# Moving an untaken path's transfers to another engine, and two steps inside a kernel's tail

## The chip, the cores and the metric

The kernel runs on one core of one Trainium2 chip. The metric is the device time of one execution in microseconds (us), given as the median of three timed runs. A profile of one more execution shows what each engine did: PE (TensorE), DVE (VectorE), ACT (ScalarE), POOL (GpSimd) and SP (SyncE), which only issues transfers and waits. Every engine has an instruction stream of its own; they meet through semaphores.

## The reference

Block-sparse attention, and behind it a layer with softmax times its input, a layer norm and a product. With q, k, v of 4 batches x 8 heads x 768 x 64, and x of 3072 tokens x 512:

```python
mask = |blk_i - blk_j| <= 1, or first or last block, or a sampled block   # blocks of 32
attn = softmax(where(mask, q @ k.T / 8, -1e9));  x = attn @ v             # heads side by side
h = x @ w_in                                       # 512 -> 1024
solu = h * softmax(h)
ln = (solu - mean(solu)) / sqrt(var(solu) + 1e-6) * g_ln
out = ln @ w_out                                   # 1024 -> 512, float32
```

## The kernel before

**The fast path.** The work is cut into 12 passes of two tiles of 128 queries over all heads. In each pass PE makes scores (L416), ACT takes the exponential without a maximum (L427), PE multiplies with v and a column of ones (L444), DVE divides (L457, L458). The 24 tiles of 128 tokens then go through the layer: PE makes h (L487), ACT e = exp(h) with its sum (`e_exp`, L496), DVE solu = h * e (`solu`, L508), the statistics of solu in two halves (`stats`, L522), and the small steps es, mv and vpe (`rstd`, L529, L532, L538); POOL raises vpe to the power -1/2 (L540). PE multiplies the turned solu by a centred w_out (L547), ACT or DVE scales the product by rstd (`scaled`) and a transfer stores it (`store`, L563).

**The order.** Nothing here is ordered by a scheduler. Each step is put into a list with a due time by `at`, and `emit` issues the list sorted by time; each engine's queue has that order. The end of the kernel, from `end`, is a list written out by hand (L937 to L973): its entries are issued one after the other. In it, pass LP - 1 is the last but one and LP the last; each has tiles 0 and 1. The last tile (LP, 1) is the end of the chain: `solu`, the turn by PE (`ln_mm`, L877), the copy (`ln_out`), the product in two halves of 256 columns (`o_half`, L893: `oe1a` and `oe1b`, eight matmuls each), the scaling of the halves by DVE and ACT (`scale_half`, L905 and L902), and two stores, one issued by SP and one by ACT.

**The flag.** The fast path is right only where no sum leaves a range. `check_r` and `check_e` (L915, L916) compare the reciprocals and the sums of all tiles with bounds, `check_sum` counts what is in range (L926) and makes `bad` (L927), one value for each partition; `check_bad` adds these up with a matmul of one column (L932, float32) and DVE writes the sum as an integer, `bad_i` (L933).

**The If.** All five engines load `bad_i` into a register (L985) and compare it with zero (L986):

```python
n_bad = nc.values_load(bad_i[0:1, 0:1], min_val=0, max_val=128)
with tc.If(n_bad > 0):
    general_path(tc, q, k, v, sampled_blocks, w_in_sb, w_out_sb, ident, out)
```

With these inputs the flag is zero, and every engine branches past its part of `general_path`, a slow version of the whole computation in loops (L57 to L205). Behind it stand waits and resets of semaphores (also L986), the wait of SP for all semaphores, and the barriers that end the program (L1012). L1001 is the start: a few register moves and fills, and a barrier that POOL opens.

Of the kernel before, what the change touches and what calls it, by code (L numbers as in the profile page):

```python
# [7 lines left out]
FP32 = mybir.dt.float32  # L8
# [7 lines left out]
def block_mask(nc, m_sb, m_ps, sampled_blocks, NB, neg):  # L16

    NR = sampled_blocks.shape[1]
    maskT = m_sb.tile([NB, NB], FP32, name="maskT")
    nc.vector.memset(maskT, 0.0)  # L20
    for fill, base, cm, step in (
        (neg, 1, -1, 1), (neg, 1, 1, -1),
        (0.0, -1, 1, 0), (0.0, NB - 2, -1, 0),
        (0.0, -1, 0, 1), (0.0, NB - 2, 0, -1),
    ):
        nc.gpsimd.affine_select(out=maskT, in_=maskT, compare_op=ALU.is_ge, fill=fill,
                                base=base, channel_multiplier=cm, pattern=[[step, NB]])
    _t = sampled_blocks.tensor
    _t32 = bass.DRamTensorHandle(_t.name, (2 * NB * NR,), I32)
    samp_flat_ap = bass.AP(tensor=_t32, offset=0, ap=[[0, 1], [1, 2 * NB * NR]])  # L30
    samp_i = m_sb.tile([1, NB * NR, 2], I32, name="samp_i")
    nc.sync.dma_start(out=samp_i.rearrange("a b c -> a (b c)"), in_=samp_flat_ap)
    ones1 = m_sb.tile([1, NB], BF16, name="ones1")
    nc.vector.memset(ones1, 1.0)
    samp_lo_bf = m_sb.tile([1, NB * NR], BF16, name="samp_lo_bf")
    nc.vector.tensor_copy(out=samp_lo_bf, in_=samp_i[:, :, 0])
    samp_ps = m_ps.tile([NB, NB, NR], FP32, name="samp_ps")
    nc.tensor.matmul(samp_ps.rearrange("a b c -> a (b c)"), ones1, samp_lo_bf,
                     start=True, stop=True)
    samp_f = m_sb.tile([NB, NB, NR], FP32, name="samp_f")  # L40
    nc.scalar.copy(out=samp_f, in_=samp_ps)
    kb_iota_i = m_sb.tile([NB, 1], I32, name="kb_iota_i")
    nc.gpsimd.iota(kb_iota_i, pattern=[[0, 1]], base=0, channel_multiplier=1)
    kb_iota = m_sb.tile([NB, 1], FP32, name="kb_iota")
    nc.vector.tensor_copy(out=kb_iota, in_=kb_iota_i)
    eq = m_sb.tile([NB, NB, NR], FP32, name="eq")
    nc.vector.tensor_scalar(out=eq, in0=samp_f, scalar1=kb_iota, scalar2=None, op0=ALU.is_equal)
    anyeq = m_sb.tile([NB, NB], FP32, name="anyeq")
    nc.vector.reduce_sum(out=anyeq, in_=eq, axis=AX.X)
    nc.vector.tensor_scalar(out=anyeq, in0=anyeq, scalar1=-1.0, scalar2=1.0,  # L50
                            op0=ALU.mult, op1=ALU.add)
    nc.vector.tensor_scalar(out=anyeq, in0=anyeq, scalar1=0.0, scalar2=None, op0=ALU.max)
    nc.vector.tensor_mul(out=maskT, in0=maskT, in1=anyeq)
    return maskT


def general_path(tc, q, k, v, sampled_blocks, w_in_sb, w_out_sb, ident, out):  # L57

    nc = tc.nc
    B, H, S, D = q.shape  # L60
    BLK = 32
    NB = S // BLK
    TQ = 128
# [3 lines left out]
    KD, KF, d_ff = w_in_sb.shape[1], w_out_sb.shape[1], w_in_sb.shape[2]  # L67
    with tc.tile_pool(name="f_c", bufs=1) as f_c, \
         tc.tile_pool(name="f_dram", bufs=1, space=bass.MemoryType.DRAM) as f_dram:
        x_scr = f_dram.tile([B, S, H * D], BF16, name="x_scr")  # L70
        m_scr = f_dram.tile([NB, S], BF16, name="m_scr")
        qT = f_c.tile([TQ, TQ], BF16, name="f_qT")
        kT = f_c.tile([TQ, S], BF16, name="f_kT")
        with tc.tile_pool(name="f_m", bufs=1) as f_m, \
             tc.tile_pool(name="f_mp", bufs=1, space=bass.MemoryType.PSUM) as f_mp:
            maskT = block_mask(nc, f_m, f_mp, sampled_blocks, NB, -1e30)
            sel = f_m.tile([NB, NB, BLK], FP32, name="sel")
            nc.vector.memset(sel, 0.0)
            nc.gpsimd.affine_select(out=sel, in_=sel, compare_op=ALU.not_equal, fill=1.0,
                                    base=0, channel_multiplier=1, pattern=[[-1, NB], [0, BLK]])  # L80
            for t in (qT, kT):
                nc.vector.memset(t[D:TQ, :], 0.0)
            nc.vector.tensor_copy(out=kT[D : D + NB, :].rearrange("p (q o) -> p q o", o=BLK),
                                  in_=sel)
            m_row = f_m.tile([NB, NB, BLK], BF16, name="m_row")
            nc.vector.tensor_copy(
                out=m_row,
                in_=maskT.rearrange("p (q o) -> p q o", o=1).broadcast_to([NB, NB, BLK]))
            nc.sync.dma_start(out=m_scr, in_=m_row.rearrange("p q o -> p (q o)"))
        with tc.tile_pool(name="f_sb", bufs=2) as f_sb, \  # L90
             tc.tile_pool(name="f_ps", bufs=1, space=bass.MemoryType.PSUM) as f_ps:
            with tc.For_i(0, B, 1) as b:
                with tc.For_i(0, H, 1) as h:
                    kc = f_sb.tile([TQ, NCH, D], BF16, tag="f_k")
                    vc = f_sb.tile([TQ, NCH, D], BF16, tag="f_v")
                    for dst, src in ((kc, k), (vc, v)):
                        nc.gpsimd.dma_start(
                            out=dst, in_=src[bass.ds(b, 1), bass.ds(h, 1), :, :].rearrange(
                                "a e (c p) d -> p (a e c) d", p=TQ))
# [5 lines left out]
                    with tc.For_i(0, S, TQ) as t0:  # L105
                        qc = f_sb.tile([TQ, D], BF16, tag="f_q")
                        nc.gpsimd.dma_start(
                            out=qc, in_=q[bass.ds(b, 1), bass.ds(h, 1), bass.ds(t0, TQ), :].rearrange(
                                "a e p d -> p (a e d)"))
                        nc.sync.dma_start(out=qT[D : D + NB, :], in_=m_scr[:, bass.ds(t0, TQ)])  # L110
                        tq = f_ps.tile([D, TQ], BF16, tag="f_tq")
                        nc.tensor.matmul(tq, qc, ident, is_transpose=True, start=True, stop=True)
                        nc.vector.tensor_copy(out=qT[0:D, :], in_=tq)
# [1 line left out]
                        for i in range(2):  # L115
                            nc.tensor.matmul(sp[:, i, 0:384], qT, kT[:, i * 384 : (i + 1) * 384],
                                             start=True, stop=True)
# [5 lines left out]
                        p = f_sb.tile([TQ, 2, 384], BF16, tag="f_p")  # L123
# [12 lines left out]
                        for j in range(NCH):  # L136
# [4 lines left out]
                        xo = f_sb.tile([TQ, D], BF16, tag="f_x")  # L141
                        nc.vector.tensor_scalar(out=xo, in0=op, scalar1=rs, scalar2=None,
                                                op0=ALU.mult)
                        nc.sync.dma_start(
                            out=x_scr[bass.ds(b, 1), bass.ds(t0, TQ), bass.ds(h * D, D)].rearrange(
                                "a p d -> p (a d)"),
                            in_=xo)
# [1 line left out]
        with tc.tile_pool(name="f_sb2", bufs=2) as f_sb, \  # L149
             tc.tile_pool(name="f_ps2", bufs=1, space=bass.MemoryType.PSUM) as f_ps:  # L150
            with tc.For_i(0, n_tok, 128) as t0:
                xt = f_sb.tile([128, d_model], BF16, tag="f_xt")
                nc.sync.dma_start(out=xt, in_=x_rows[bass.ds(t0, 128), :])
                tps = f_ps.tile([128, KD, 128], BF16, tag="f_tps")
                for c in range(KD):
                    nc.tensor.matmul(tps[:, c, :], xt[:, c * 128 : (c + 1) * 128], ident,
# [45 lines left out]
                                     stop=(c == KF - 1))  # L202
                ot = f_sb.tile([128, d_model], FP32, tag="f_ot")
                nc.scalar.copy(out=ot, in_=ops)
                nc.sync.dma_start(out=out[bass.ds(t0, 128), :], in_=ot)  # L205


@with_exitstack
def kernel(
# [11 lines left out]
    nc = tc.nc  # L221
# [5 lines left out]
    TQ = 128  # L227
# [346 lines left out]
    with tc.manual_schedule():  # L574
# [309 lines left out]

        o2 = {}

        def o_half(half, pool, tag):
            if pool is p_sco:
                o2[half] = p_sco.tile([128, 2, HF], FP32, tag=tag, name="oe1a")[:, 0, 0:256]
            else:  # L890
                o2[half] = pool.tile([128, d_model], FP32, tag=tag, name="oe1b")[:, 0:256]
            for c in range(KF):
                nc.tensor.matmul(o2[half], lnT_of[LP, 1][:, c, :],  # L893
                                 w_cen_sb[:, c, half * 256 : (half + 1) * 256],
                                 start=(c == 0), stop=(c == KF - 1), skip_group_check=True)
# [13 lines left out]
        def tile_in(pool, tag, name):  # L909
            if pool is p_sco:  # L910
                return lambda: p_sco.tile([128, 2, HF], FP32, tag=tag, name=name)[:, 0, :]
            return lambda: pool.tile([128, d_model], FP32, tag=tag, name=name)
# [12 lines left out]
        def check_sum():  # L925
            nc.vector.reduce_sum(out=n_ok[:, 0:1], in_=okr, axis=AX.X)  # L926
            nc.vector.tensor_scalar(out=bad, in0=n_ok[:, 0:1], scalar1=float(n_r + n_e),  # L927
                                    scalar2=None, op0=ALU.is_lt)

        def check_bad():  # L930
            bad_ps = p_h.tile([1, 1], FP32, tag="h", name="bad_ps")
            nc.tensor.matmul(bad_ps, bad, ones_c, start=True, stop=True)  # L932
            nc.vector.tensor_copy(out=bad_i, in_=bad_ps)  # L933

        end = SLOTS * NPASS
        A, V = nc.scalar, nc.vector
        for n, (fn, *args) in enumerate((  # L937
            (h_end, 0, 2, KD),
            (e_exp, LP, 0),
            (o_mms, LP - 1, 0, 5, 8),  # L940
            (scaled, LP - 1, 0, A),
            (store, LP - 1, 0),
            (stats, LP - 1, 1),
            (rstd, LP - 1, 1),
            (check_r, n_r - 2 * PC, n_r),
            (h_end, 1, 0, KD),
            (solu, LP, 0),
            (e_exp, LP, 1),
            (o_mms, LP - 1, 1, 0, 3, tile_in(p_op, "op", "o_10")),
            (ln_mm, 0),  # L950
            (ln_out, 0, A),
            (o_mms, LP - 1, 1, 3, 8),
            (solu, LP, 1),
            (check_e,),
            (stats, LP, 0),
            (rstd, LP, 0),
            (o_mms, LP, 0, 0, 2, tile_in(p_sco, "sco", "oe0")),
            (ln_mm, 1),
            (ln_out, 1, A),
            (stats, LP, 1),  # L960
            (rstd, LP, 1),
            (o_mms, LP, 0, 2, 8),
            (scaled, LP - 1, 1, A),
            (store, LP - 1, 1),
            (check_sum,),
            (scaled, LP, 0, A),
            (store, LP, 0),
            (o_half, 0, p_sco, "sco"),
            (o_half, 1, p_op, "op"),
            (scale_half, 0, V, nc.sync),  # L970
            (scale_half, 1, A, nc.scalar),
            (check_bad,),
        )):  # L973
            at(end + 0.01 * n, fn, *args)
        at(end - 5.0, x_turn, LP, 0, 2)
# [41 lines left out]
```

## Time and profile before

| | us |
|---|---|
| timed runs | 213.96 median (213.76 to 214.35) |
| the profiled execution | 213.1 |
| its span, first to last instruction | 211.5 |
| PE, ACT, DVE, POOL busy | 199.9, 174.5, 139.9, 107.4 |
| granted clock of PE, mean | 0.989 |

The span leaves out what lies around the program in an execution. Of a row of a timeline, the first number is the start in us from the span's start, the second the duration; square brackets hold the idle time of the engine before it and what ended it. A "q" behind an engine's name is its sequencer: waits, branches, register loads and the issuing of transfers, which aren't counted as busy. In rows that list one line, "17/30/43" is the shortest, median and longest duration in ns, and two start times follow. EVENT_SEMAPHORE is a wait, a reset, or both; it is recorded when it is done, with some 20 ns. DMA queues q8 and q14 hold the fetches of instructions.

### The profile page before, as it was taken

Reading aid. Unit: us, or ns where it says so; the run is one execution under the profiler, and the core shown is the slowest. Engines: PE = TensorE matmul, PEld = TensorE weight load, DVE = VectorE, ACT = ScalarE, POOL = GpSimd, SP = SyncE. Lnnn points to the kernel's source line nnn. Section 1 sums busy time; section 2 is a strip of 40 time slices with the busy share of each in tenths; the row PEclk is TensorE's granted clock in tenths of the full one; section 3 lists DMA queues with packets and bytes.
Section 4 is the critical chain, followed back from the end, with each engine's and each line's share of the span. In section 5 each row is a group of like instructions: output and inputs, shape, how many; then the busy total and the mean of one; then the engine's idle time right before and its main releaser. Section 6 shows DMA issues by size and latency. Waiting matters only on the chain.

```text
span 211.5 us, 5629 instructions
## 1 busy us (share of the span) xinstructions
PE 199.9 (95%) x2238; PEld 137.5 (65%) x2238; DVE 139.9 (66%) x329; ACT 174.5 (82%) x208; POOL 107.4 (51%) x155
## 2 busy tenths in 40 slices
PE   7989999999989999999999999999999999999950
PEld 2669867776666677677667667567667667664530
DVE  5895879988647656656655755756745845768760
ACT  6988989889869889889888988888988988784640
POOL 7989698679494264689334355699111011011120
PEclk9999999999999999999999999999999999999995
DMA  6999999899999799997798899896706507462230
GB/s 173 338 360 217 379 376 273 166 243 271 194 301 203 180 258 237 274 192 203 193 299 154 189 311 261 199 269 127 206 3 149 81 24 124 125 83 76 79 149 11
DMA packets 73907, 42.03 MB, mean 199 GB/s; under 512 B 55828, under 2 KB 69396, under 8 KB 73876
## 3 DMA queue, kind: packets, MB, share of 16 engines
q1 hardware_dynamic: 72932, 40.06, 77.9%
q0 software_dynamic: 528, 1.05, 2.6%
q10 hardware_dynamic: 416, 0.52, 0.9%
q8 instruction: 18, 0.29, 0.6%
q14 instruction: 13, 0.11, 0.2%
HBM read 23.07 MB, written 6.29 MB: 139 GB/s over the span
## 4 chain that ended last, share of the span: by engine, by line
PE 74%; DVE 8%; DMA 7%; POOL 3%; issue 2%; ACT 2%; ACTq 0%; POOLq 0%; DVEq 0%
PE sco L416 25%; PE h L487 15%; PE op L444 15%; PE o L547 13%; DMA pd<-nat 5%; DMA xT<-xb 2%; DVE stats L522 2%; POOL KT L327 2%; PE warm_t L403 2%; DVE solu L508 2%; PE he L867 1%; DVE QT L664 1%; POOL QT L327 1%; PE mean_ps L750 1%; PE tp_k L346 1%
## 5 line engine op out<-in xcount | busy, mean ns | idle before, releaser
L427 ACT ACTIVATE exs<-sco 128x1024 bf16<-128x1024 f32 x144 | 140.4, 1024 | 9.4 <-PE sco L416 6.9
L416 PE MATMUL sco<-QT,KT 88*128 88x256 bf16 x576 | 86.9, 272 | 1.1 <-POOL QT L327 0.5
L416 PEld LDWEIGHTS <-KT 88*128 88x128 bf16 x576 | 54.2, 97 | 32.9 <-issue 6.6
L487 PE MATMUL h<-w_in_sb,xT 128*128 128x512 bf16 x176 | 55.3, 379 | 0.3 <-DMA xT<-xb 0.3
L444 PE MATMUL op<-VA,exs 128*128 128x65 bf16 x1152 | 51.8, 194 | 0.0
L444 PEld LDWEIGHTS <-exs 128*128 128x128 bf16 x1152 | 48.5, 97 | 3.7 <-DVE xb L458 0.3
L547 PE MATMUL o<-w_cen_sb,lnT 128*128 128x512 bf16 x176 | 45.2, 379 | 0.0
L540 POOL TENSOR_TENSOR rstd<-vpe,mhalf 128x1 f32<-128x1 f32 x24 | 13.2, 548 | 54.9 <-DVE vpe L538 49.5
L457 DVE RECIPROCAL recip_all<-op 128x4 f32<-128x4 f32 x48 | 8.7, 182 | 42.8 <-PE op L444 42.7
L496 ACT ACTIVATE e<-h 128x1024 bf16<-128x1024 f32 x22 | 22.5, 1023 | 12.9 <-PE h L487 11.5
L522 DVE BATCH_NORM_STATS2 stats<-solu 128x6 f32<-128x512 bf16 x48 | 30.6, 680 | 0.0
L327 POOL COPY KT<-pd 64x768 bf16<-64x768 bf16 x24 | 20.1, 837 | 16.5 <-DMA pd<-nat 15.7
L508 DVE TENSOR_TENSOR solu<-h,e 128x1024 bf16<-128x1024 f32 x22 | 26.8, 1216 | 1.6 <-ACT e L496 1.6
L547 PEld LDWEIGHTS <-lnT 128*128 128x128 bf16 x176 | 15.9, 98 | 13.8 <-DMA lnT<-solu 0.2
L558 DVE TENSOR_SCALAR ot<-o,rstd 128x512 f32<-128x512 f32 x20 | 15.0, 751 | 10.8 <-issue 5.3
L458 DVE TENSOR_TENSOR xb<-op,recip_all 128x256 bf16<-128x256 f32 x48 | 20.4, 424 | 1.7
L327 POOL COPY QT<-pd 64x768 bf16<-64x768 bf16 x24 | 19.7, 821 | 1.0
L487 PEld LDWEIGHTS <-xT 128*128 128x128 bf16 x176 | 16.0, 98 | 5.2 <-DMA xT<-xb 1.5
L327 POOL CAST nat<-st_q 128x768 bf16<-128x768 f32 (+2 forms) x19 | 13.6, 714 | 8.1 <-DMA st_q<-in_q_dram 8.0
L327 POOL CAST VA<-st_v 128x768 bf16<-128x768 f32 x16 | 13.1, 828 | 7.7 <-DMA st_v<-in_v_dram 3.9
L327 POOL CAST nat<-st_k 128x768 bf16<-128x768 f32 x15 | 12.7, 846 | 4.9 <-DMA st_k<-in_k_dram 4.6
L740 POOL TENSOR_SCALAR w_out_sb<-w_out_f,g_ln_sb 128x512 bf16<-128x512 f32 x8 | 6.0, 759 | 2.1 <-DMA w_out_f<-in_moe_w_out_dram 2.1
(89 smaller groups left out, 113.5 us busy)
## 6 DMA issues: line engine op xcount, KB each, us to landing
st_v<-in_v_dram SPq DMA_DIRECT2D x16, 384.0 KB, 5.0
out_dram<-ot SPq DMA_DIRECT2D x23, 256.0 KB, 2.6
st_k<-in_k_dram SPq DMA_DIRECT2D x15, 384.0 KB, 5.5
st_q<-in_q_dram SPq DMA_DIRECT2D x12, 384.0 KB, 6.5
w_out_f<-in_moe_w_out_dram SPq DMA_DIRECT2D x4, 512.0 KB, 7.6
st_q<-in_q_dram SPq DMA_DIRECT2D x4, 256.0 KB, 6.9
w_in_sb<-in_moe_w_in_dram POOLq DMA_DIRECT2D x1, 1024.0 KB, 11.9
st_q<-in_q_dram SPq DMA_DIRECT2D x4, 128.0 KB, 4.7
```

The lines of the kernel that those rows point to most:

```text
L327: eng.tensor_copy(out=o, in_=i)
L416: nc.tensor.matmul(sco[:, hh, kk * QW : (kk + 1) * QW], KT[b % 2][0:KR, h * NCH + 2 * u + kk, :], QT[b % 2][0:KR, h * NCH + PC * j : h * N ...
L427: nc.scalar.activation(out=exs_of[ps, pr][:, u].rearrange("p a b c -> p (a b c)"), in_=sco_of.pop(s).rearrange("p a b -> p (a b)"), func=A ...
L444: nc.tensor.matmul(op[:, hh, ic, :], exs[:, u, hh, kk, ic * TQ : (ic + 1) * TQ], VA[b % 2][:, 2 * pr + hh, 2 * u + kk, :], start=(u == 0 a ...
L458: nc.vector.tensor_tensor(out=xb_of[ps][:, pr].rearrange("p c (h d) -> p h c d", h=2), in0=op[:, :, :, 0:D], in1=recip.broadcast_to([TQ, 2 ...
L487: nc.tensor.matmul(h_of[ps, i][:, half, :], xT_of[ps][:, c * PC + i, :], w_in_sb[:, c, half * HF : (half + 1) * HF], start=(c == 0), stop= ...
L496: nc.scalar.activation(out=o, in_=h, func=ACT.Exp, scale=1.0, accum_out=esum_all[:, t : t + 1])
L508: nc.vector.tensor_mul(out=so, in0=h, in1=e)
L522: nc.vector.bn_stats(out=stat_of[ps, i][:, half, :], in_=so[:, half, :])
L540: nc.gpsimd.tensor_tensor(out=rstd_of[ps, i], in0=vpe, in1=mhalf, op=ALU.pow)
L547: nc.tensor.matmul(ops_of[ps, i], lnT_of[ps, i][:, c, :], w_cen_sb[:, c, :], start=(c == 0), stop=(c == KF - 1), skip_group_check=True)
L558: nc.vector.tensor_scalar(out=o, in0=i_, scalar1=r, scalar2=None, op0=ALU.mult)
```

## The change

Three edits.

1. Six transfers of `general_path` and `block_mask` are issued by POOL instead of SP: the sampled blocks, the mask's two, the loop's store of x, the second loop's load and its store. They aren't executed with these inputs.
2. In the list of the end, the statistics of tile (LP, 0) go ahead of the last `solu`, the steps of its rstd follow that solu at once, then the statistics and rstd of the last tile, then `check_e` and `check_sum`.
3. `check_bad` is cut in two: its matmul stands between the fifth and the sixth matmul of `oe1b`, and the copy to `bad_i` behind DVE's scaled half.

```diff
-    nc.sync.dma_start(out=samp_i.rearrange("a b c -> a (b c)"), in_=samp_flat_ap)
+    nc.gpsimd.dma_start(out=samp_i.rearrange("a b c -> a (b c)"), in_=samp_flat_ap)
...
-            nc.sync.dma_start(out=m_scr, in_=m_row.rearrange("p q o -> p (q o)"))
+            nc.gpsimd.dma_start(out=m_scr, in_=m_row.rearrange("p q o -> p (q o)"))
...
-                        nc.sync.dma_start(out=qT[D : D + NB, :], in_=m_scr[:, bass.ds(t0, TQ)])
+                        nc.gpsimd.dma_start(out=qT[D : D + NB, :], in_=m_scr[:, bass.ds(t0, TQ)])
...
-                        nc.sync.dma_start(
+                        nc.gpsimd.dma_start(
                             out=x_scr[bass.ds(b, 1), bass.ds(t0, TQ), bass.ds(h * D, D)].rearrange(
...
-                nc.sync.dma_start(out=xt, in_=x_rows[bass.ds(t0, 128), :])
+                nc.gpsimd.dma_start(out=xt, in_=x_rows[bass.ds(t0, 128), :])
...
-                nc.sync.dma_start(out=out[bass.ds(t0, 128), :], in_=ot)
+                nc.gpsimd.dma_start(out=out[bass.ds(t0, 128), :], in_=ot)
...
-        def o_half(half, pool, tag):
-            if pool is p_sco:
+        def o_half(half, pool, tag, c0=0, c1=KF):
+            if c0:
+                pass
+            elif pool is p_sco:
...
-            for c in range(KF):
+            for c in range(c0, c1):
...
         def check_bad():
-            bad_ps = p_h.tile([1, 1], FP32, tag="h", name="bad_ps")
-            nc.tensor.matmul(bad_ps, bad, ones_c, start=True, stop=True)
-            nc.vector.tensor_copy(out=bad_i, in_=bad_ps)
+            bad_ps.append(p_h.tile([1, 1], FP32, tag="h", name="bad_ps"))
+            nc.tensor.matmul(bad_ps[0], bad, ones_c, start=True, stop=True)
+
+        def check_out():
+            nc.vector.tensor_copy(out=bad_i, in_=bad_ps[0])
...
             (solu, LP, 0),
+            (stats, LP, 0),
             (e_exp, LP, 1),
             (o_mms, LP - 1, 1, 0, 3, tile_in(p_op, "op", "o_10")),
             (ln_mm, 0),
             (ln_out, 0, A),
             (o_mms, LP - 1, 1, 3, 8),
             (solu, LP, 1),
-            (check_e,),
-            (stats, LP, 0),
             (rstd, LP, 0),
+            (stats, LP, 1),
             (o_mms, LP, 0, 0, 2, tile_in(p_sco, "sco", "oe0")),
             (ln_mm, 1),
             (ln_out, 1, A),
-            (stats, LP, 1),
             (rstd, LP, 1),
+            (check_e,),
+            (check_sum,),
             (o_mms, LP, 0, 2, 8),
             (scaled, LP - 1, 1, A),
             (store, LP - 1, 1),
-            (check_sum,),
             (scaled, LP, 0, A),
             (store, LP, 0),
             (o_half, 0, p_sco, "sco"),
-            (o_half, 1, p_op, "op"),
+            (o_half, 1, p_op, "op", 0, 5),
+            (check_bad,),
+            (o_half, 1, p_op, "op", 5, KF),
             (scale_half, 0, V, nc.sync),
+            (check_out,),
             (scale_half, 1, A, nc.scalar),
-            (check_bad,),
```

Lines behind the diff's third part are two to eight higher after: L915 is L917, L893 is L895, L932 is L936, L933 is L939, L985 is L993, L986 is L994, L1012 is L1020.

What the compiled programs hold between an engine's branch at the If and its target, and behind the target to the end, counted in their lists of instructions:

| | passed over, before | after | behind the target, before | after |
|---|---|---|---|---|
| SP | 137 | 110 | 21 | 17 |
| POOL | 126 | 154 | 11 | 14 |
| DVE | 128 | 136 | 5 | 5 |
| ACT | 105 | 113 | 5 | 5 |
| PE | 197 | 205 | 5 | 5 |

The program's start differs too: register moves ahead of the first barrier are four on SP and three on POOL before, none and five after. At the end SP's list of waits for semaphores has ten entries before and twelve after, POOL's waits at the If two and five; the six that SP has at the If before are gone after.

More of the change, by code (lines that the diff above doesn't have):

```diff
@@ L928, in check_sum @@
                                     scalar2=None, op0=ALU.is_lt)
+        bad_ps = []
         def check_bad():
-            bad_ps = p_h.tile([1, 1], FP32, tag="h", name="bad_ps")
-            nc.tensor.matmul(bad_ps, bad, ones_c, start=True, stop=True)
-            nc.vector.tensor_copy(out=bad_i, in_=bad_ps)
+            bad_ps.append(p_h.tile([1, 1], FP32, tag="h", name="bad_ps"))
+            nc.tensor.matmul(bad_ps[0], bad, ones_c, start=True, stop=True)
+        def check_out():
+            nc.vector.tensor_copy(out=bad_i, in_=bad_ps[0])
         end = SLOTS * NPASS
```

## The prediction

> **What bounds the kernel now.** I read the page first, for the span, then the timeline of the last ten microseconds, then the rows of the lines that end the program. From the page:
>
> ```profile
> span 211.5 us, 5629 instructions
> ```
>
> The profiled execution took 213.1 us, 1.6 us more than its span, and the median of the three timed runs is 213.96. I make the sum against the span and take what it changes from the median.
>
> The change touches the first half microsecond, the last ten, and a path that isn't run. Up to 195 us both kernels issue the same work in the same order, so the end is where to look. The timeline there, cut to what the argument needs (start, duration, engine, line, operation):
>
> ```profile
> 196.12 1.22 DVE L508 TENSOR_TENSOR solu<-he,e 128x1024 bf16<-128x1024 f32 x1 [0.15 <-ACT e L496]
> 198.50 1.23 DVE L508 TENSOR_TENSOR solu<-he,e 128x1024 bf16<-128x1024 f32 x1 [1.15 <-ACT e L496]
> 199.84 0.18 DVE L916 SCALAR_TENSOR_TENSOR okr<-esum_all,okr 128x24 f32<-128x24 f32 x1
> 199.94 1.28 DVE L522 BATCH_NORM_STATS2 stats<-solu 128x6 f32<-128x512 bf16 x2
> 201.50 0.16 DVE L538 TENSOR_TENSOR vpe<-es,mv 128x1 f32<-128x1 f32 x1
> 201.57 1.28 DVE L522 BATCH_NORM_STATS2 stats<-solu 128x6 f32<-128x512 bf16 x2
> 202.57 1.04 PE L893 MATMUL oe1b<-w_cen_sb,lnTe 128*128 128x256 bf16 x8
> 203.20 0.16 DVE L538 TENSOR_TENSOR vpe<-es,mv 128x1 f32<-128x1 f32 x1
> 203.28 0.37 DVE L926 TENSOR_REDUCE n_ok<-okr 128x1 f32<-128x216 f32 x1
> 203.50 0.55 POOL L540 TENSOR_TENSOR rstd<-vpe,mhalf 128x1 f32<-128x1 f32 x1 [1.16 <-DVE vpe L538]
> 203.68 0.15 DVE L927 TENSOR_SCALAR bad<-n_ok 128x1 f32<-128x1 f32 x1
> 203.98 0.19 PE L932 MATMUL bad_ps<-ones_c,bad 128*1 128x1 f32 x2 [0.38 <-DVE bad L927]
> 204.09 0.47 ACT L902 ACTIVATE ot_last<-oe1b,rstd 128x256 f32<-128x256 f32 x1 [1.02 <-POOL rstd L540]
> 204.09 0.48 DVE L905 TENSOR_SCALAR ot_last<-oe1a,rstd 128x256 f32<-128x256 f32 x1 [0.25 <-POOL rstd L540]
> 204.49 0.13 DVE L933 CAST bad_i<-bad_ps 1x1 int32<-1x1 f32 x1
> 204.59 0.38 ACTq L563 DMA_DIRECT2D out_dram<-ot_last  x1
> 204.60 0.33 SPq L563 DMA_DIRECT2D out_dram<-ot_last  x1
> ```
>
> DVE runs without a gap from 198.50 to 203.84; the last tile's rstd ends at 204.05 because two pairs of statistics stand behind the last solu. PE has finished the last product at 203.61, and ACT stands idle 1.02 us for rstd. So up to 204.6 DVE's queue is the limit. But 6.9 us of span are left, and in them no engine computes. The waits of SP's own queue, then the rows of line 986 (the If), of the two register loads that count, and of line 1012 (the end of the program):
>
> ```profile
> SPq L986 <- SPq L986: 3.6, 1, 3.6
> ```
>
> ```profile
> L986 SPq EVENT_SEMAPHORE  x6: 17/17/17, 209.5 to 209.9; - x6
> L986 POOLq EVENT_SEMAPHORE  x2: 17/30/43, 205.7 to 205.8; - x2
> L986 POOLq COMPARE_BRANCH  x1: 45/45/45, 205.2 to 205.2; - x1
> L986 DVEq COMPARE_BRANCH  x1: 72/72/72, 205.3 to 205.3; - x1
> L986 ACTq COMPARE_BRANCH  x1: 54/54/54, 205.7 to 205.7; - x1
> L986 DVEq EVENT_SEMAPHORE  x1: 21/21/21, 205.9 to 205.9; - x1
> L986 SPq COMPARE_BRANCH  x1: 53/53/53, 205.9 to 205.9; - x1
> L986 POOLq INC_SWDGE_SEM  x1: 206/206/206, 205.9 to 205.9; - x1
> L986 ACTq EVENT_SEMAPHORE  x1: 17/17/17, 206.2 to 206.2; - x1
> ```
>
> ```profile
> L985 POOLq TENSOR_LOAD <-bad_i x1: 503/503/503, 204.7 to 204.7; - x1
> L985 SPq TENSOR_LOAD <-bad_i x1: 544/544/544, 205.0 to 205.0; - x1
> ```
>
> ```profile
> L1012 SPq EVENT_SEMAPHORE  x12: 17/28/28, 210.0 to 211.5; - x12
> L1012 SPq DRAIN  x3: 7/7/13, 210.6 to 211.0; - x3
> ```
>
> Every engine loads the flag, branches past the general path and goes on behind it. POOL, DVE and ACT are there 0.5 us after their branch. **SP branches at 205.9 and does its next instruction at 209.5.** It waits for no transfer: stores take at most 2.0 us to land, so the one issued at 204.59 is in by 206.6.
>
> ```profile
> DMA to landing us min/median/max: 1.8/2.0/2.0
> ```
>
> From 210.0 SP walks ten waits in 0.6 us, 0.06 each; then 0.9 us of barriers end the span. What sets the end is SP's jump.
>
> The DMA view, for 204.5 to 207.6 us (two rows) and for 207.6 to the end (one), shows what runs meanwhile:
>
> ```profile
> q14 instruction: 4, 0.03, 4.1%
> q8 instruction: 1, 0.02, 2.3%
> ```
>
> ```profile
> q14 instruction: 1, 0.01, 0.5%
> ```
>
> Five instruction fetches follow the five jumps; a sixth comes alone near SP's resumption. That fits a jump that left what SP had loaded, so that it had to wait for its target. The lengths fit too: the jumps of ACT, POOL and DVE pass over 105, 126 and 128 instructions (the table in the section on the change) and cost 0.5 us or less, SP's passes over 137 and costs 3.6. Fetches on q14 are 8 KB each (0.03 MB in four), on q8 16 KB. How many instructions that is, two lines of the page tell:
>
> ```profile
> PE   199.9 (95%) x2238; PEld 137.5 (65%) x2238; DVE 139.9 (66%) x329; ACT 174.5 (82%) x208; POOL 107.4 (51%) x155
> q8 instruction: 18, 0.29, 0.6%
> ```
>
> Only PE has a program so long: its 4476 instructions in 18 fetches make about 250 for 16 KB, so about 125 for 8 KB.
>
> **The change part by part.** *Transfers of the general path.* None is executed, so none costs time as a transfer. What moves is program length: SP's jump shrinks from 137 to 110 instructions, POOL's grows from 126 to 154, DVE's from 128 to 136. SP's 110 is near ACT's 105, so I take its jump at 0.5 us (bounds 0.4 and 3.6). POOL's 154 isn't in the trace: from below 0.4, its own jump of 126; from above 3.6, SP's of 137. It lies nearest, and beyond, the jump that stalled, so **I take 3.6 us on POOL**. DVE's 136 is one short of 137; I take 3.6 there as well, hidden as shown below.
>
> [...]
>
> *Start.* SP issues register moves ahead of the first barrier, and POOL issues three; POOL gets two more and SP loses its four.
>
> ```profile
> L1001 SPq MOVE  x4: 29/34/42, 0.0 to 0.2; - x4
> L1001 POOLq MOVE  x3: 29/29/39, 0.1 to 0.3; - x3
> ```
>
> POOL's moves start some 0.06 apart, and POOL opens the barrier: +0.1 us on everything (bounds 0 and 0.2).
>
> *Statistics ahead of the last solu.* The first solu ends at 197.34. Its statistics, 1.28, now fill the gap in which DVE waited for e: 197.4 to 198.65. The last solu can start some 0.08 before that end, as pipelined neighbours do here: 198.57 instead of 198.50. PE's last products shift by this 0.07 (bounds 0 and 0.2). Behind the solu come es, mv and vpe of the last but one tile (0.45), then the last tile's statistics from 200.15, es, mv, vpe (201.77 in place of 203.20): **rstd 1.43 us earlier**, 202.07 to 202.62. The checks of esum (0.4), the reduce and the comparison follow, and bad is there near 202.8 (before: 203.83).
>
> *The flag's sum inside the last products.* PE reaches it after five of eight matmuls of oe1b, near 203.2, so bad is 0.4 us early; if it were late, three matmuls and ACT's store would wait with it. The two f32 matmuls delay those three by 0.05 to 0.25; I take 0.15. oe1b ends near 203.83, ACT scales at once and issues its store at 204.36 in place of 204.59. DVE's half needs rstd and oe1a, whose last matmul ends with oe1b's first ones (202.8): scaled by 203.33, SP's store at 203.35 in place of 204.60. bad_i is written by 203.57, in place of 204.62: 1.05 earlier.
>
> *The end, added up.* POOL's load starts 0.04 after bad_i: 203.62, branch done at 204.2. With the stall it goes on at 207.8. It then has five waits where it had two, at about 0.09 each, and INC_SWDGE_SEM: 0.7, to 208.5. SP has been behind its own branch since 205.2 but its first end wait is for a semaphore that this instruction raises. Twelve waits of 0.06 follow (0.75), then 0.9: 210.15, and 210.25 with the start. DVE, if it stalls, is back at 207.9; the last store has landed by 206.4; both lie under POOL. The span changes by 210.25 - 211.5 = -1.25 us. From the median: **212.7 us**.
>
> **The rivals.**
>
> *No jump stalls.* What counts would be how many block ends lie within the jump, and not its length. With blocks of about 125 a jump of 137 passes two ends in some 12 positions of 125, one of 154 in some 29: POOL would be spared in three of four cases. For it: the fetches come in whole blocks. Against it: that SP had one of 12 positions in 125 would be chance, whereas length explains all four rows. [...] The end is then the last store, landed at 206.4; SP has seven waits left (0.45), then 0.9 and 0.1: 207.85, 3.65 us less, 210.3 us. If DVE alone stalled, SP would meet its semaphore at 207.9: five waits, 0.9 and 0.1 give 209.2, 211.7 us.
>
> *SP stalls all the same (the move does nothing).* The cause would be something else that only SP has, such as the two operations of line 985 between load and branch. Its flag load follows its store, 203.7 rather than 205.0; the branch ends at 204.7, it is back at 208.3, twelve waits, 0.9 and 0.1: 210.05, -1.45, 212.5 us.
>
> *Slower: POOL stalls twice.* POOL has some fourteen instructions behind its target. If a block ends within them, the next block is asked for only at resumption (the lone sixth fetch stands near SP's resumption, too), and POOL pays a second 3.6 ahead of its INC_SWDGE_SEM, with SP and the barrier behind it: -1.25 + 3.6 = +2.35, 216.3 us. It decides from the point where a second stall costs more than 1.25 us. Against it: 14 positions of 125, and SP with 21 instructions behind its target shows one stall.
>
> **How the numbers follow.** POOL stalls once: 0.55. No stall 0.25, with DVE alone in it. SP stalls all the same 0.09. POOL twice 0.05. The rest, 0.06, is for a tail that gives back what I count, about no change. The range 209.9 to 213.3 holds the first three, with 0.4 us on either side for the starting moves, PE's two matmuls and a stall a little longer than SP's, and leaves out 0.11 to 0.2. About 0.3% (0.64 us) is what a measurement of this kernel can tell from no change; the forecast's -1.25 lies beyond it, and needs a stall of over 4.2 us to fall inside. Faster 0.86, same 0.08, slower 0.06.
>
> **What would show it.** Line 994 (the If) after: SP's waits begin 0.5 us after its branch, or they don't; POOL's first wait stands 3.6 us after POOL's branch, or 0.4; DVE's likewise. rstd of the last tile ends near 202.7, bad_i near 203.7, ACT's last store starts near 204.5 (each with the 0.1 of the start). SP's end waits begin near 208.6. If POOL doesn't stall I am wrong by 2.4 us to the long side; if bad comes after PE's fifth matmul, PE has a gap ahead of line 936.

## The result, and the profile after

| | before | after |
|---|---|---|
| median of seven runs, us | 213.96 (213.15 to 214.98) | 211.82 (210.41 to 212.45) |
| ratio after/before | | 0.9884, 95% interval 0.9848 to 0.9919 |
| the profiled execution, us | 213.1 | 210.96 |
| its span, us | 211.5 | 209.2 |

The kernel became 1.2% faster by the ratio, which is that of the means; by the medians it is 1.0%. The forecast said 212.7 in a range of 209.9 to 213.3, so the time lies where it was expected; the way there was another one. Page of the profile after, its first line:

```profile
span 209.2 us, 5592 instructions
```

The If after the change (line 994; it was 986):

```profile
L994 POOLq EVENT_SEMAPHORE  x5: 17/43/43, 204.8 to 205.2; - x5
L994 POOLq COMPARE_BRANCH  x1: 45/45/45, 204.4 to 204.4; - x1
L994 DVEq COMPARE_BRANCH  x1: 72/72/72, 204.4 to 204.4; - x1
...
L994 SPq COMPARE_BRANCH  x1: 53/53/53, 204.7 to 204.7; - x1
...
L994 DVEq EVENT_SEMAPHORE  x1: 21/21/21, 205.0 to 205.0; - x1
L994 POOLq INC_SWDGE_SEM  x1: 195/195/195, 205.2 to 205.2; - x1
```

POOL branches at 204.4 and does its next instruction at 204.8; DVE takes 0.6 us. **No jump stalls**, though POOL's passes over 154 instructions. SP's waits at the If are gone; what it does behind its branch stands in the row of the program's end, and its waits tell where it stood longest:

```profile
L1020 SPq EVENT_SEMAPHORE  x14: 17/28/28, 205.4 to 209.2; - x14
...
L1020 SPq DRAIN  x3: 7/7/13, 208.4 to 208.7; - x3
```

```profile
SPq L1020 <- DMA out_dram<-ot_last: 2.2, 1, 2.2
SPq L1020 <- PEq L1020: 0.7, 2, 0.5
SPq L1020 <- remote: 0.6, 1, 0.6
```

The 0.6 us on `remote` end when POOL's INC_SWDGE_SEM is done (205.2 and 0.195 us). SP begins its end waits then, at 205.4, and could be through by 206.1. It stands 2.2 us in one of them, for a store of `ot_last`, until 207.9; seven waits and the barriers follow. So the last store ends this kernel. When was it issued? The tail's timeline:

```profile
202.00 0.57 POOL L540 TENSOR_TENSOR rstd<-vpe,mhalf 128x1 f32<-128x1 f32 x1 [1.15 <-DVE okr L917]
...
202.61 0.15 DVE L929 TENSOR_SCALAR bad<-n_ok 128x1 f32<-128x1 f32 x1
...
203.13 0.19 PE L936 MATMUL bad_ps<-ones_c,bad 128*1 128x1 f32 x2
...
203.26 0.50 PE L895 MATMUL oe1b<-w_cen_sb,lnTe 128*128 128x256 bf16 x3
203.27 0.33 SPq L563 DMA_DIRECT2D out_dram<-ot_last  x1
203.36 0.15 DVE L939 CAST bad_i<-bad_ps 1x1 int32<-1x1 f32 x1
203.84 0.47 ACT L904 ACTIVATE ot_last<-oe1b,rstd 128x256 f32<-128x256 f32 x1 [1.14 <-issue]
204.35 0.37 ACTq L563 DMA_DIRECT2D out_dram<-ot_last  x1
```

ACT issues it at 204.35 and it lands at 207.9, 3.5 us later; before, the same store was issued at 204.59 and landed at 206.62 by the trace's landing records, 2.0 us later. The transfers of the changed kernel in two stretches, 205.45 to 206.4 and 206.4 to 207.9 us (packets, MB, share of the 16 DMA engines). q10 is ACT's queue, which carries only this store here, in 128 packets of 1 KB and 16 of 4 bytes; q14 and q8 carry instructions:

```profile
q10 hardware_dynamic: 70, 0.06, 19.2%
q14 instruction: 4, 0.03, 12.9%
q8 instruction: 1, 0.02, 7.8%
```

```profile
q10 hardware_dynamic: 15, 0.01, 7.0%
```

Five instruction fetches, as many as there are jumps, run among the store's packets from 205.49 on, and 15 packets start only when all five fetches have started (the fifth at 206.38), the last at 207.3. In the kernel before, the same two queues between 205.6 and 206.3, and between 206.3 and 207.6:

```profile
q10 hardware_dynamic: 144, 0.13, 53.9%
```

```profile
q14 instruction: 4, 0.03, 9.8%
q8 instruction: 1, 0.02, 5.4%
```

There all 144 packets are through, the last at 206.28, before the first fetch starts at 206.35. In the changed kernel bad_i comes at 203.51 in place of 204.62, the first branch at 204.36 in place of 205.23, the first fetch at 205.49 in place of 206.35, and so among the packets of the store.

### The profile page after: what moved, and what is told of

Same layout as the page of the kernel before. It is cut to its first block, busy times and chain, and to the rows that moved or that the text cites. A ratio compares the mean times of both kernels' runs of the same rounds, so it can differ in the third digit from the quotient of the medians.

```text
span 209.2 us, 5592 instructions
## 1 busy us (share of the span) xinstructions
PE 198.0 (95%) x2204; PEld 137.3 (66%) x2238; DVE 140.1 (67%) x329; ACT 174.7 (84%) x208; POOL 107.7 (51%) x155
## 4 chain that ended last, share of the span: by engine, by line
PE 71%; DMA 9%; POOL 8%; DVE 5%; issue 3%; ACT 1%; POOLq 0%
PE sco L416 24%; PE op L444 15%; PE o L547 13%; PE h L487 13%; DMA pd<-nat 7%; POOL KT L327 3%; DMA xT<-xb 2%; POOL QT L327 2%; PE he L867 1%; POOL nat L670 1%; DVE QT L664 1%; PE oe L547 1%; PE mean_ps L750 1%; DVE xb L458 1%; POOL nat L327 1%
## 5 line engine op out<-in xcount | busy, mean ns | idle before, releaser
L487 PE MATMUL h<-w_in_sb,xT 128*128 128x512 bf16 x153 | 48.6, 378 | 0.7 <-DMA xT<-xb 0.2
L547 PE MATMUL o<-w_cen_sb,lnT 128*128 128x512 bf16 x166 | 43.2, 379 | 0.5
L327 POOL CAST nat<-st_q 128x768 bf16<-128x768 f32 (+2 forms) x19 | 14.3, 752 | 9.8 <-DMA st_q<-in_q_dram 9.4
L327 DVE COPY QT<-tp_q 64x256 bf16<-64x256 bf16 (+1 forms) x16 | 5.6, 351 | 1.4 <-PE tp_q L356 1.1
```

The source lines that it names most:

```text
L327: eng.tensor_copy(out=o, in_=i)
L487: nc.tensor.matmul(h_of[ps, i][:, half, :], xT_of[ps][:, c * PC + i, :], w_in_sb[:, c, half * HF : (half + 1) * HF], start=(c == 0), stop= ...
L547: nc.tensor.matmul(ops_of[ps, i], lnT_of[ps, i][:, c, :], w_cen_sb[:, c, :], start=(c == 0), stop=(c == KF - 1), skip_group_check=True)
```

## The experiments

Two questions were open. When does a jump stall: by its **length** (the forecast's reading), or by **how many ends of fetch blocks lie within it** (the first rival)? And why does the store land late: by the **collision** with the fetches, or for something in the tail or in the moved transfers?

For the first, block ends have to be placed. No record shows one; as an estimate, an end is put where an 8 KB fetch starts in mid-run. In the trace of before a q14 fetch starts at 75.2 us, where SP stands at about the 80th instruction of its list; POOL's fetch at 147.8 us gives about 195 in the same way. With 126 instructions for 8 KB (two such fetches stand 126 apart in e8, below; 4476 instructions of PE in 18 fetches of 16 KB, from the page of before, give 124), SP's ends lie near 81, 207 and 333, POOL's near 195, 321 and 447. SP's jump before (from 201 to 339) passes two, SP's after (197 to 308) one, POOL's after (217 to 372) one. These places are worked out; the runs test them. At one of them a fetch can also be seen. In e3, e8 and e9 below SP has 20 instructions more ahead of the If, and one more fetch starts on q14 between 194 and 196 us, with SP at its 208th or 209th instruction, 126 behind the place of its first fetch; before has none there. In e4, with 88 more on POOL, the fetch that before has at 147.8 us, with POOL at its 196th instruction, comes at 97.2, with POOL at its 198th. The ends at 333, 321 and 447 lie in the part that isn't run, and stay worked out. From e8, 195 to 197 us:

```profile
q14 instruction: 1, 0.01, 1.3%
```

The executions of one kernel differ by up to 2 us in when the tail begins (e1 and r2 in the table), so that the traces are compared from the issue of ACT's last store on; the times are medians. This table holds all kernels, in us; "fetches" is the first instruction fetch behind the If, "packets" the start of the store's last packet of 1 KB, both from the trace's records of packets.

| kernel | store issued | fetches | packets | end of span | end less issue | median | ratio to before, 95% |
|---|---|---|---|---|---|---|---|
| before | 204.59 | 206.35 | 206.22 | 211.5 | 6.9 (SP stalls) | 213.96 | 1 |
| changed | 204.35 | 205.49 | 207.29 | 209.2 | 4.9 | 211.82 | 0.9884 (0.9848 to 0.9919) |
| e1_transfers_only | 204.87 | 206.67 | 206.50 | 208.3 | 3.4 | 209.84 | 0.9844 (0.9804 to 0.9884) |
| e2_tail_only | 206.11 | 207.28 | 209.96 | 212.6 | 6.5 (SP stalls) | 213.03 | 0.9945 (0.9924 to 0.9965) |
| e3_sp_padded | 207.42 | 209.22 | 209.05 | 211.2 | 3.8 | 211.86 | 0.9911 (0.9882 to 0.9940) |
| e4_pool_padded | 206.00 | 207.02 | 209.24 | 212.3 | 6.3 (POOL stalls) | 212.45 | 0.9931 (0.9906 to 0.9955) |
| e5_flag_late | 204.62 | 206.41 | 205.94 | 208.0 | 3.3 | 209.64 | 0.9837 (0.9792 to 0.9883) |
| e6_sum_last | 204.46 | 206.10 | 205.78 | 207.7 | 3.2 | 209.69 | 0.9817 (0.9777 to 0.9858) |
| e7_no_branch | 204.77 | none | 206.09 | 207.5 | 2.7 | 209.36 | 0.9788 (0.9752 to 0.9825) |
| e8_sp_padded_later | 205.61 | 207.36 | 207.24 | 209.4 | 3.8 | 210.32 | 0.9831 (0.9793 to 0.9869) |
| e9_tail_sp_padded | 204.72 | 205.81 | 208.24 | 209.9 | 5.2 | 212.37 | 0.9930 (0.9899 to 0.9960) |
| r1_changed_again | 204.77 | 205.92 | 208.33 | 210.2 | 5.5 | 211.53 | 0.9894 (0.9858 to 0.9931) |
| r2_transfers_again | 206.81 | 208.55 | 208.44 | 210.3 | 3.4 | 209.91 | 0.9813 (0.9781 to 0.9844) |
| r3_sum_last_again | 204.20 | 205.84 | 205.52 | 207.4 | 3.2 | 209.20 | 0.9796 (0.9762 to 0.9829) |

e1 to e4 shared one chip; e5 to e8, and later the last four, shared another. The before beside them took 213.84, 213.60 and 213.78.

### e1_transfers_only: the change's first part alone

All six lines of the change's first part, beside the kernel before:

```diff
-            nc.sync.dma_start(out=m_scr, in_=m_row.rearrange("p q o -> p (q o)"))
+            nc.gpsimd.dma_start(out=m_scr, in_=m_row.rearrange("p q o -> p (q o)"))
...
-                nc.sync.dma_start(out=out[bass.ds(t0, 128), :], in_=ot)
+                nc.gpsimd.dma_start(out=out[bass.ds(t0, 128), :], in_=ot)
```

> Only the general path's transfers go to GpSimd; the tail is that of the kernel before. Theory of places (a jump stalls if two ends of an 8 KB fetch block lie inside it, whatever its length): SP goes from instruction 197 to 308 and passes one end (near 207), POOL from 217 to 372 and passes one (near 321), so SP's waits begin 0.5 us behind its branch and no jump stalls. The flag comes 1.05 us later than in the changed kernel, so the fetches start near 206.4, behind the packets of the last store, which lands by 206.7: SP's end waits begin near 206.8, span 208.2 (before 211.5, changed 209.2), some 3.3 us less than before, and so faster than the changed kernel. Theory of length: POOL's 154 stalls 3.6 us: span 211 or more. Rival, that the tail's edits carry the 2.3 us: span 211.5 as before.

Span 208.3. The kernel with the first of the three edits alone has a lower median than the whole, 209.84; the intervals of the two ratios overlap, and r1 and r2 below settle it on one chip. No jump stalls, the fetches start 0.17 us behind the store's last packet, and 3.4 us behind the issue all is over. Length falls here, unless POOL's jump is special.

### e2_tail_only: the change's second and third part alone

Against the changed kernel, all six transfers back on SP:

```diff
-            nc.gpsimd.dma_start(out=m_scr, in_=m_row.rearrange("p q o -> p (q o)"))
+            nc.sync.dma_start(out=m_scr, in_=m_row.rearrange("p q o -> p (q o)"))
...
-                nc.gpsimd.dma_start(out=out[bass.ds(t0, 128), :], in_=ot)
+                nc.sync.dma_start(out=out[bass.ds(t0, 128), :], in_=ot)
```

> Only the tail's edits; the general path's transfers stay on SP, whose jump goes from 201 to 339 as before. Places and length agree: SP stalls for 3.6 us behind a branch near 204.7, back at 208.3; the last store lands late or not, it is hidden under the stall; twelve waits and the barriers: span 210.1 to 210.3, 1.3 us less than before. Rival, that the tail carries the gain: span 209.2 as changed, with SP's waits from 205.3.

SP's waits, in us in total, times, longest:

```profile
SPq L994 <- SPq L994: 4.2, 1, 4.2
```

SP stalls again, for 4.2 us in this execution, and the profiled execution began its tail 1.8 us late (the store's issue at 206.11, the changed kernel's at 204.35), so that its span of 212.6 isn't that of the forecast. The median fell by 0.8 us, less than the 1.3 expected. A stall of 4.2 in place of 3.6 would account for the difference, if the timed runs have it too, which no profile of them shows. In the packets the collision is there and hidden: fetches from 207.28, the store's last packet at 209.96, 3.9 us behind its issue.

### e3_sp_padded: SP's jump moved by 20 instructions, length as before

Beside the kernel before:

```diff
+    pad = const_pool.tile([1, 64], FP32)
+    def pad_sp(n):
+        nc.sync.dma_start(out=pad[:, n : n + 1], in_=moe_g_ln[n : n + 1].rearrange("(p o) -> p o", o=1))
...
+        for n in range(20):
+            at(60.0 + n, pad_sp, n)
```

> The kernel before, with 20 loads of 4 bytes each on SP's queue in the middle of the run. They go into a buffer that nothing reads; SP's jump keeps its 137 instructions and all its operations, but goes from 221 to 359 in place of 201 to 339. Theory of places: one block end (near 333) is left inside it, the stall goes, SP's waits begin 0.5 us behind its branch, span 208.2. Theory of length, or of something that SP's jump alone has: 3.6 us behind the branch, span 211.5.

SP at the If (line 993 in this kernel):

```profile
L993 SPq EVENT_SEMAPHORE  x6: 17/17/17, 209.3 to 209.7; - x6
...
L993 SPq COMPARE_BRANCH  x1: 53/53/53, 208.7 to 208.7; - x1
```

The jump is still 137 instructions long, over the same operations, and SP is back after 0.5 us where it was back after 3.6. **Length falls**, and so does anything else in SP's program that the jump skips or that stands between load and branch. The median missed the forecast's 3.3 us (2.0 less than before): PE waited 1.5 us near 90 us, as the waits of PE from 86 to 94 us show. The 20 loads shared that stretch with the turning transfers, which may be why; it isn't shown, for in e4, without these loads, PE waits 0.8 us at the same place.

```profile
PE h L492 <- DMA xT<-xb: 1.5, 1, 1.5
```

### e8_sp_padded_later: the same loads, placed past 150 us

```diff
-            at(60.0 + n, pad_sp, n)
+            at(108.0 + n, pad_sp, n)
```

> The kernel before with the 20 small loads on SP placed where SP issues little, past 150 us, so that they don't meet the transposing transfers near 90 us. SP's jump goes from 219 to 357, still over 137 instructions, past one block end (near 333). Theory of places: no stall, SP's waits 0.5 us behind its branch, the last store lands ahead of the fetches; span and time 3.2 us less than before, near 210.6. Theory of length: 213.9.

```profile
SPq L993 <- SPq L993: 0.5, 1, 0.5
```

Median 210.32, 3.3 less than before on its chip: twenty loads that nobody needs, and the stall is gone. This is the price of the stall by itself; in the traces, from the issue of the last store to the end, it is 3.1 (6.9 and 3.8 in the table).

### e4_pool_padded: POOL's jump moved by 88 instructions

Beside the changed kernel:

```diff
+    pad = const_pool.tile([1, 64], FP32)
+    def pad_pool(n):
+        nc.gpsimd.memset(pad[:, n % 64 : n % 64 + 1], 0.0)
...
+        for n in range(88):
+            at(40.0 + 0.5 * n, pad_pool, n)
```

> The changed kernel, with 88 memsets of one element on POOL between 60 and 130 us, whose results nothing reads. POOL's jump keeps its 154 instructions, but goes from 305 to 460 in place of 217 to 372. Theory of places: two block ends (near 321 and 447) lie inside it, so that POOL stalls some 3.6 us behind its branch near 204.3: its first wait at 208, INC_SWDGE_SEM at 208.6, SP's end waits from 208.7, span 210.3 (the changed kernel 209.2). Rival, that only SP stalls in such a jump: POOL's first wait 0.4 us behind its branch, span 209.2 with the same late store.

POOL at the If (line 1001 here), and SP's longest wait:

```profile
L1001 POOLq EVENT_SEMAPHORE  x5: 17/43/43, 210.0 to 210.4; - x5
L1001 POOLq COMPARE_BRANCH  x1: 45/45/45, 206.0 to 206.0; - x1
```

```profile
SPq L1027 <- remote: 4.2, 1, 4.2
```

The same 154 instructions that POOL jumped in 0.4 us now cost it **4.0**, with the jump moved, by the places worked out, from over one end to over two. This is the stall that the forecast put on POOL; it came where the place asked for it. The profiled execution entered the tail 1.65 us later than the changed kernel's, which the expected 210.3 didn't hold; the median is 0.6 to 0.9 us above the two medians of the changed kernel (the intervals overlap, so that the trace decides here), with the late store hidden under the stall: it landed at 209.76, ahead of POOL's return.

### e5_flag_late: the flag 0.75 us later

Beside the changed kernel:

```diff
+        def check_late(n):
+            for _ in range(n):
+                nc.vector.reduce_sum(out=n_ok[:, 1:2], in_=okr, axis=AX.X)
...
             (scale_half, 0, V, nc.sync),
+            (check_late, 3),
             (check_out,),
```

> The changed kernel with three more sums of okr (0.29 to 0.37 us each, into a column that nothing reads) on DVE ahead of the copy of the flag, so that bad_i comes 0.75 us later, near 204.25. Theory of collision (the instruction fetches of the jumps, which start 1.1 us behind the branches, met the packets of ACT's last store, which run from 0.9 to 1.4 us behind its issue at 204.35): the branches come near 204.9, the fetches from 206.0, behind the packets (205.3 to 205.8), the store lands by 206.4, SP's end waits run on POOL's semaphore from 206.1: span 207.8 by more work and a later flag, 1.4 us less than the changed kernel. Rival, that the flag's path is what ends last: 0.75 us more, span 209.9. Rival, that the store lands late for a reason in the tail itself: landed at 207.9 again, span 209.2.

With three idle sums ahead of the flag the kernel has a median of 209.64, some 2 us under the changed kernel's two; the intervals of the ratios overlap in part. The first branch comes 0.65 us behind the store's issue in place of 0.01. The trace tells why: span 208.0, no stall, the fetches 0.47 us behind the last packet. Both rivals are out: the flag's path doesn't end last in the changed kernel, and this same tail lands its store in 1.7 us (issue 204.62, landed 206.3).

### e6_sum_last: without the change's third part

Beside the changed kernel:

```diff
             (o_half, 0, p_sco, "sco"),
-            (o_half, 1, p_op, "op", 0, 5),
-            (check_bad,),
-            (o_half, 1, p_op, "op", 5, KF),
+            (o_half, 1, p_op, "op"),
             (scale_half, 0, V, nc.sync),
-            (check_out,),
             (scale_half, 1, A, nc.scalar),
+            (check_bad,),
+            (check_out,),
```

> The changed kernel with the flag's sum behind the last products again (transfers on GpSimd and early statistics stay). The three last matmuls lose their 0.15 us gap, ACT's store is issued near 204.2, bad_i is there near 204.2. Theory of collision: fetches from 206.0, store's packets 205.1 to 205.7, landed by 206.3: span 207.7, faster than the changed kernel and than the transfers alone (208.3). Theory that the earlier flag is worth its place: 0.7 us more than the changed kernel, 209.9.

As expected: span 207.7. Putting the flag's sum among the last products was worth less than nothing (r1 and r3 below put a number on it). SP's waits here, as in e5 and r3, hold 0.7 us for POOL's semaphore (`remote`) and none for the store: without the collision the flag's way through POOL is what ends last.

```profile
SPq L1019 <- remote: 0.7, 1, 0.7
```

### e7_no_branch: without the If

Beside the changed kernel; the slow path is left out, so that a flag other than zero would be without effect:

```diff
-    n_bad = nc.values_load(bad_i[0:1, 0:1], min_val=0, max_val=128)
-    with tc.If(n_bad > 0):
-        general_path(tc, q, k, v, sampled_blocks, w_in_sb, w_out_sb, ident, out)
```

> The changed kernel without the load of the flag, the If and the general path, which is left out. Theory of collision: no jump, so no fetch in the last microseconds; ACT's last store, issued at 204.35, lands by 206.4, seven waits and the barriers: span 207.7 or less. Rival, that the store lands late for a reason in the tail itself (its order, its place behind the other stores): landed at 207.9, span 209.2.

```profile
SPq L1017 <- DMA out_dram<-ot_last: 2.3, 1, 2.3
```

SP waits for the store here too, but only since it is there early: issued at 204.77, landed at 206.5, end 1.0 later. From the store's issue to the end this takes 2.7 us, the least in the table. e6 and r3, with their If, take 3.2, and their times can't be told from e7's 209.36.

### e9, r1, r2, r3: the store's neighbour, and the three versions on one chip

e9 is e2 with the loads of e8:

```diff
+        for n in range(20):
+            at(108.0 + n, pad_sp, n)
```

r1 is the changed kernel, r2 is e1 and r3 is e6, each once more.

> Transfers on SP as before, the changed tail with the flag's sum inside the last products, and the 20 small loads on SP past 150 us, so that SP's jump (219 to 357) doesn't stall. Collision: the fetches meet ACT's last store, which lands 3.4 us or more behind its issue in place of 2.0; SP waits for it, and the time is that of the changed kernel, 211.8, some 1.5 us more than with the old tail and the same loads (210.3). Rival, that the transfers on GpSimd are what makes the store late: landed 2.0 behind its issue, time 209.6.

> The changed kernel itself, beside the two versions below on one chip: 211.8 by both theories; its last store lands 3.4 us behind its issue, give or take what the collision does in this execution.

> The transfers alone, beside the changed kernel on one chip: 209.9, 1.9 us less than the changed kernel. If the two chips of the earlier runs made the difference, 211.8.

> Transfers on GpSimd, early statistics, the flag's sum last, beside the two above on one chip: 209.4, some 0.5 us less than the transfers alone (its spans were 207.7 and 208.3) and 2.3 less than the changed kernel. If the early statistics are worth nothing: 209.9.

SP's waits in e9:

```profile
SPq L1027 <- DMA out_dram<-ot_last: 2.4, 1, 2.4
SPq L1001 <- SPq L1001: 0.5, 1, 0.5
```

No stall at the jump, and the late store: 212.37 where the old tail with the same loads has 210.32. So the moved transfers have no part in it. On one chip the changed kernel takes 211.53, the transfers alone 209.91, and e6's version 209.20. The changed kernel's second profile shows the collision best. Its transfers from 206.78 to 207.65 us, and from 207.65 to 208.4:

```profile
q14 instruction: 1, 0.01, 3.7%
```

```profile
q10 hardware_dynamic: 9, 0.01, 6.5%
```

For 0.87 us no packet of the store starts. The records show why: PE's 16 KB fetch starts at 205.94 and takes 1756 ns, to 207.70; the nine packets, a sixteenth of the store, start at 207.68. In e9 that fetch ends at 207.60 and the packets start at 207.59. In all five kernels with a late store the first late packet starts as a q14 fetch ends, and the second nine begin as PE's fetch ends, each within 0.04 us (in the changed kernel 206.17 and 206.17, then 206.72 and 206.73). That fits a share of the store that waits until a fetch is through; which DMA engine carries which packet, the records here don't tell. r3, from 205.0 to 205.6 and from 205.6 to 206.8 us:

```profile
q10 hardware_dynamic: 144, 0.13, 62.5%
```

```profile
q14 instruction: 4, 0.03, 9.4%
q8 instruction: 1, 0.02, 6.5%
```

First the store, then the fetches. In the table the store's last 1 KB packet starts 1.3 to 1.6 us behind the issue in every kernel whose fetches start 1.6 us or more behind it, and 2.9 to 3.9 behind in the five whose fetches start after 1.0 to 1.2.

## Why the prediction was right in the time and wrong in a step

- **What bounds the kernel before:** right. SP's jump is the end, and taking away its stall alone (e8) gave 3.3 us.
- **The start, +0.1:** right at the start. POOL has its five moves, and the trace has ACT's first activation 0.11 later. At the tail it can't be seen any more: the last solu but one starts at 196.05, and at 196.12 before.
- **SP's jump 0.5:** right in size (0.52 in e1; in the changed kernel 0.7, from 204.7 to 205.4, with the wait for POOL in it), for another reason than the length of 110, as e3 and e8 show with 137 and 0.5; by the places worked out it passes one block end in place of two.
- **POOL's jump:** the step that failed. "It lies nearest, and beyond, the jump that stalled, so I take 3.6 us on POOL" put length in the place of position. POOL took 0.4. 137 instructions don't stall in e3, e8 and e9, and 154 do in e4. The argument against the rival, that two ends within SP's jump would be chance, was the mistake: one stalled jump among four needs no rule by length. The count of ends fits SP's and POOL's jumps in these runs, 0.4 to 0.6 us where one end is passed and 3.6 to 4.2 where two are; it is a reading from places worked out, and why two ends should stall and one not, no trace shows.
- **DVE's jump of 136:** taken as a hidden 3.6, measured 0.6; it changed nothing.
- **The tail up to the store:** right to 0.1 us, and to 0.2 if the forecast's start of 0.1 is added to each. rstd ends at 202.57 (forecast 202.62), bad is there at 202.76 (202.8), the flag's matmuls at 203.13 (203.2), the store is issued at 204.35 (204.36), SP's half at 203.27 (203.35), bad_i at 203.51 (203.57).
- **The last store:** "landed by 206.4" took 2.0 us from a trace in which no fetch met the store; it took 3.5. The first rival had the right jumps and rested on this number, which is why it came out at 210.3. With 207.9 in its place, its own sum gives 207.9 + 0.45 + 0.9 = 209.25: the span of 209.2.
- **The sum:** -1.25 us forecast, -2.1 in the medians and -2.3 in the spans. Without the stall the forecast's own sum ends 2.4 us earlier (207.85 in place of 210.25), and the late landing gives back 1.4 of that (209.25). Two mistakes cancel in part: that the time lies 0.9 us from the forecast is luck, and the range was wide enough for the first rival too.

That the stall goes with the place of the jump is shown by e3, e4 and e8 (the count of ends, with a fetch seen near SP's 207th instruction, is the reading that fits), and that the store lands late where it meets the fetches by e5, e6, e7 and e9. Of the change, the first part brings 3.9 to 4.0 us (e1, r2); the early statistics beside it 0.6 to 0.7 (e6 against e1 by their ratios, r3 against r2; the intervals overlap, so that the size stays open); the third part takes back about 2.3 on one chip (r1 against r3), and 1.4 by the ratios of the changed kernel and e6. The version without it, r3, is the fastest of the complete kernels that were run, 0.9796 of before, and its interval lies clear of the changed kernel's 0.9858 to 0.9931.

Open are three things: why a jump stalls at all, and for 3.6 us and more when a fetch on q14 takes about half a us (0.31 to 0.68 in before and the changed kernel); why, with five fetches, only 18 of the store's 144 packets came late (two groups of nine); and where the executions get the 2 us by which their tails start apart.

## What to carry to other kernels

A jump over a rarely used path stalled here or didn't by where it lay in its engine's program: 20 idle loads ahead of it took SP's stall away (e8, 3.3 us of the median), 88 idle memsets brought one of 4.0 us on POOL (e4). Before crediting an edit, look whether a branch and its target moved. What an edit makes earlier has to be followed to the transfers that it triggers: here the branches came 0.87 us earlier, the fetches 0.86, and so into the last store. Where fetches and a store meet at the end, take no landing time from a trace in which they were apart: 2.0 us in before, 3.5 in the changed kernel.

## What the runs showed of the hardware

- In these kernels the next instruction behind a taken branch came 0.4 to 0.6 us after it (POOL 0.4 and DVE 0.6 in the changed kernel, SP 0.5 in e3 and e8), or 3.6 (SP, before), 4.0 (POOL, e4) and 4.2 us (SP, e2), with as many instructions skipped (137 on SP in e3 and before, 154 on POOL in the changed kernel and e4).
- Five fetches follow the five jumps in every kernel with the If, the first 1.0 to 1.2 us behind the first branch, and none in e7, which has no If: four of 8 KB on q14 (0.35 to 0.68 us in before and the changed kernel) and one of 16 KB on q8 (1.13 in before, 1.18 in the changed kernel, 1.76 in r1). Where a jump stalls (before, e2, e4), and nowhere else within a span, a sixth follows, 0.8 us behind SP's return in before and 0.6 to 0.7 behind POOL's in e4.
- A store of 128 KB that meets them lands 3.5 to 4.4 us behind its issue (3.5 in the changed kernel, 3.8 in e4) in place of 1.7 (e5, e7), or of 2.0 where SP's store is issued beside it (before, e1, e3, e8, r2); its late packets of 1 KB take up to 0.45 us each in the changed kernel, where the others take 0.046.
